# The first product of a fused convolution and feed-forward block: 81 to 80 products a block, with a new order of all queues

## The chip, the core and the metric

The kernel runs on one core of a Trainium2 chip. The core has a matrix engine (TensorE, in the profile PE; its weight loads are PEld), three other compute engines (VectorE DVE, ScalarE ACT, GpSimd POOL) and SyncE (SP), which here issues transfers only. Each engine works through its own queue in order, and the engines wait for one another by semaphores. The metric is the device time of one execution in microseconds (us).

## The reference

`x` has 8 sequences of 4096 tokens with 192 channels. Each channel is convolved along the sequence with 7 taps (a softmax over a row of `weight`, one row for each of 8 groups of 24 channels); then follows a feed-forward block with a SiLU between two matrix products.

```python
def _attn_ref(x, weight):
    ...
    x_unf = x_pad[:, idx, :].reshape(B, S, K, H, group)
    out = np.einsum('hk,bskhg->bshg', w, x_unf)
    return out.reshape(B, S, D).astype(np.float32)

def _moe_ref(x, w_in, w_out):
    h = x @ w_in                          # 32768 x 192 by 192 x 2048
    g = h * (1.0 / (1.0 + np.exp(-h)))
    return (g @ w_out).astype(np.float32) # by 2048 x 192
```

Everything is in 32-bit floats.

## The kernel before

**Blocks.** The 32768 tokens are cut into 32 blocks (`NB`) of 1024 (`TT`), and each block into two halves of 512 (`TB`). The 192 channels are three thirds of 64 (`NK`), and the 2048 hidden features are 16 chunks of 128. Block 0 is computed plainly (`up_plain`, `down_plain`); from block 1 on, both matrix products are computed with fewer multiplications, in the manner of Strassen's scheme: sums of inputs and sums of weights are multiplied, and the results are sums of these products.

**Up products (h).** One product is a matmul with 64 rows (a third of the channels, or a sum of such thirds), 128 columns (a chunk of features, or a sum of chunks) and 512 tokens; it occupies one half of TensorE's rows, the upper or the lower one, and a product in the other half can run beside it. Plainly, a block needs 16 x 3 x 2 = 96 of them. Before, the chunks stand in five groups of three (`GROUPS`), each with 15 products in place of 18, and one chunk stays plain (`plain`, two of its products cut into halves of 256 tokens): 5 x 15 + 6 = 81. `product` adds into one of three banks of a group (`CHAINS`, `CHAIN_BANKS`); `sums_h` makes the outputs out of them: ScalarE copies a bank (`u`), VectorE adds (`X`, `a`, `b`), ScalarE takes the SiLU (`S`).

**Inputs of the up products.** `load` (token `ld`) brings a third of the channels of a block's tokens into `nat` with four transfers of 64 KB; `turn_in` (`i`) transposes it on VectorE into `xt`; `halo_in` (`ha`) fills in the six tokens before each half, with a transfer `xt<-xt` among its steps; `conv` (`v`) computes the taps, the first on ScalarE and six on VectorE, back into `nat`; `spread` (`sp`) copies the result within the chip's SBUF to both halves of the rows (`dup`, eleven transfers a block); `win` (`w`) makes the sums of inputs (six VectorE adds).

**Down products.** `out_slot` (`D`) multiplies with 128 rows and 32 columns, four such tiles side by side, 192 matmuls a block; `sum_g` (`t`) makes its sums of inputs on VectorE (16 a block), `merge` (`z`, `y`, `x`, `M`) its sums of outputs, `turn_out` (`o`) transposes the output on VectorE, `store_out` (`st`) stores it, three transfers of 64 KB each.

**The order.** Nothing is scheduled while the kernel is built: two lists of tokens are written out, `START` for the first blocks and `PLAN` for all others, and every instruction is pinned to its place in its engine's queue (`pin`). `step` reads a token: `P8.3` is product 8 of group 3 of block b; a prefix moves it to another block (`-` one back, `=` two back, `+` one ahead). `ld`, `i`, `ha`, `v`, `sp`, `w` always work for the block after the one named. `PLAN` is gone through 31 times, for b from 3 to 33; what is not there any more is left out. In the old `PLAN`, 48 `D` tokens stand in one stretch, and the products in another. Its input steps stand thus (number of `P` and `L` tokens and of `D` tokens ahead of them): `+ld.1` 0 and 0, `+ld.2` 2 and 13, `+i.2` 19 and 48, `+ld.0` 29 and 48, `+i.1` 48 and 48, `+i.0` 61 and 48.

**Weights.** `combine` makes the sums of weights of a group once, on GpSimd, each operation on 64 rows and 128 columns (19 for a group, 3 more for one of them).

Of the kernel before, what the change touches and what calls it, by code (L numbers as in the profile page):

```python
# [9 lines left out]
F32 = mybir.dt.float32  # L10
# [7 lines left out]
def kernel(  # L18
# [8 lines left out]

# [4 lines left out]
    nc = tc.nc  # L43
# [33 lines left out]

    PLAN = (
        "+ld.1 P5.0 | -P8.3 -S1.4 -a0.2 -S4.3 | -D0.00 -t.01 -S0.2 | -D1.00 -S1.2 =o.2 v.00 "
        "| -D2.01 -t.03 -S5.1 =st.2 | -D2.00 -b5.3 | -D1.20 -sp.0 v.21 -S5.3 | -D4.01 u5.0 "
        "-t.02 -S1.3 | -D5.01 -sp.2 | -D4.00 -t.10 | -D0.20 -t.11 | -D3.01 | -D0.11 -t.12 | "
        "-D1.30 v.22 | -D3.00 +ld.2 -t.13 | -D2.11 -a0.3 | -D5.00 | -D2.10 -t.20 -S0.3 | "
        "-D3.11 v.11 | -D5.10 | -D4.11 -w.0 | -D0.30 v.12 | -D4.10 -t.21 | -D1.11 -t.23 | "
        "-D0.21 | -D0.01 v.23 -w.1 | -D3.10 -t.22 | -D5.21 | -D0.31 | -D5.11 | -D1.10 -t.30 "
        "| -D1.01 -t.31 | -D2.20 | -D2.21 v.13 | -D5.20 | -D4.21 v.01 v.14 | -D4.20 v.24 | "
        "-D1.21 -w.2 | -D3.20 -t.33 | -D2.30 v.02 | -D1.31 -t.32 | -D2.31 -y1.0 | -D5.30 "
        "v.03 | -D0.10 v.25 | -D3.21 -z1.0 v.15 -y0.0 | -D4.31 -y2.0 -w.3 | -D5.31 -M1.0 | "  # L90
        "-D3.30 -x2.1 v.26 -x2.0 | -D4.30 -x2.2 -M2.0 | -D3.31 -w.5 -x0.0 -M3.0 | L.02 | "
        "P2.0 -x2.3 -w.4 | P5.4 | P3.0 u4.0 -M6.0 | L.12 v.16 u5.4 | L.00 | P6.0 -x1.0 -M4.0 "
        "| L.10 u2.0 | P2.4 | L.01 X2.0 | L.11 v.04 u4.4 | P9.0 | P1.0 SL.0 -M5.0 SL.2 | "
        "P6.4 | P13.0 u0.0 X4.0 SL.1 | P5.1 | P3.4 -M7.0 S2.0 +i.2 u2.4 | P0.0 | P7.0 X2.4 | "
        "P11.0 | P12.0 u1.0 a5.0 -o.1 | P9.4 | P1.4 S4.0 b1.0 -st.1 u5.1 | P13.4 | P4.0 X4.4 "
        "u0.4 | P10.0 | P2.1 a1.0 +ld.0 v.05 | P7.4 | P0.4 u4.1 b5.0 | P14.0 | P8.0 u1.4 "
        "v.06 S5.0 | P11.4 | P14.4 a5.4 S3.0 a0.0 S2.4 | P6.1 | P12.4 S3.4 | P4.4 | P3.1 "
        "u2.1 b1.4 S4.4 | P5.2 | P10.4 X2.1 | P1.1 a1.4 u5.2 | P9.1 b5.4 | P2.2 u0.1 | P8.4 "
        "X4.1 | P5.3 u4.2 | P7.1 a0.4 | P0.1 +i.1 u5.3 sp.1 | P12.1 a5.1 | P6.2 u1.1 | P3.2 "
        "-o.0 | P4.1 u2.2 b1.1 | P13.1 | P2.3 a1.1 | P10.1 S2.1 | P1.2 u4.3 X2.2 | P8.1 | "  # L100
        "P11.1 -o.3 u0.2 | P13.2 S1.1 a0.1 | P6.3 S4.1 | P9.2 +i.0 | P0.2 b5.1 u2.3 +ha.0 | "
        "P3.3 S0.0 X4.2 | P1.3 S2.2 | P12.2 u1.2 | P11.2 X2.3 | P7.2 u0.3 b1.2 | P14.1 S4.2 "
        "| P9.3 a5.2 S0.4 | P0.3 -st.0 | P10.2 S1.0 X4.3 | P14.2 u1.3 | P7.3 b5.2 +v.20 "
        "-st.3 | P4.2 S0.1 | P12.3 a5.3 S3.1 | P14.3 +v.10 a1.2 | P13.3 | P4.3 S5.2 b1.3 | "
        "P8.2 S2.3 | P11.3 a1.3 S3.3 | P10.3 S5.4 t.00 S3.2"
    )
    START = (
        "=dp.28 =v.20 =v.10 =dp.44 =v.00 =dp.18 =dp.6 =dp.40 =dp.7 =dp.32 =dp.23 =dp.30 "
        "=dp.13 =dp.2 =dp.20 =dp.24 =dp.15 =dp.35 =dp.14 =dp.33 =dp.11 -ld.1 =dp.37 =dp.36 "
        "=dp.25 -ld.2 =dp.27 =dp.17 -ld.0 =dp.0 =v.11 =dp.34 =v.01 =dp.26 =v.12 =dp.29 =v.21 "  # L110
        "=v.13 =dp.45 =v.22 =dp.21 =v.02 =dp.42 =v.14 =v.03 =dp.39 =v.15 =dp.3 =v.04 =dp.38 "
        "=v.16 =dp.47 =v.23 =sp.1 =v.05 =dp.1 =v.24 =dp.22 -i.1 =dp.12 =v.25 =v.06 =dp.43 "
        "=v.26 =go.2 =sp.0 =dp.19 -i.0 =dp.46 -i.2 =dp.31 -ha.0 =dp.9 =sp.2 =dp.4 =dp.41 "
        "-v.10 -v.00 -v.11 =dp.8 -v.20 -v.01 =dp.5 -v.12 =dp.16 -v.02 =w.0 =dp.10 =w.1 =cp.0 "
        "-L.01 -P5.0 -v.03 =cp.1 -L.02 -P5.4 =w.2 -u5.0 -L.10 =w.3 -u5.4 -P2.0 -P3.0 -v.13 "
        "-P2.4 -u4.0 -v.04 -P6.0 -L.00 -u4.4 -L.12 -u2.0 -L.11 -SL.0 -X2.0 -P6.4 -SL.2 =w.4 "
        "=cp.2 -P9.0 -P1.0 -u2.4 =o.0 -P13.0 -P5.1 -v.14 -u0.0 -X4.0 -P3.4 -P1.4 -S2.0 =w.5 "
        "-SL.1 -P7.0 -P11.0 -u5.1 -X2.4 -u0.4 -P12.0 -P0.0 -a5.0 -v.21 -P13.4 -P0.4 -u1.0 "
        "=o.1 -P4.0 -P9.4 -u1.4 -v.15 -S4.0 -P2.1 -P14.4 -a1.0 -b1.0 -P14.0 -P8.0 -u4.1 -X4.4 "
        "-S3.4 -P6.1 -P10.0 -v.22 -S2.4 -a0.0 -P11.4 -P7.4 -u2.1 -b5.0 -S3.0 -P5.2 -P3.1 "  # L120
        "-S4.4 -a5.4 -P1.1 -P12.4 -u5.2 -X2.1 -P4.4 -u0.1 -P9.1 -b1.4 -P2.2 -a1.4 -P10.4 "
        "-X4.1 -P5.3 -u4.2 -P8.4 =o.2 -P6.2 -b5.4 -P13.1 -u5.3 =st.2 -a0.4 -P0.1 -P7.1 -u2.2 "
        "-v.23 -S2.1 ld.1 -P2.3 -P3.2 -a5.1 -u1.1 -S0.0 -P1.2 -P12.1 -X2.2 -S0.4 -P4.1 -u4.3 "
        "-P13.2 -b1.1 ld.2 -S1.4 -P6.3 -a1.1 -u0.2 -P10.1 -v.24 -P11.1 -u2.3 -P8.1 -b5.1 "
        "-P0.2 -S4.1 -P9.2 -v.05 -S2.2 -a0.1 -P12.2 -P1.3 -u1.2 -X4.2 -S0.1 -P3.3 -P14.1 "
        "-b1.2 -u0.3 -S5.4 -P7.2 -P11.2 -X2.3 -v.16 -P10.2 -P0.3 -S4.2 -a5.2 -sp.1 -P9.3 "
        "-P14.2 -u1.3 -b5.2 -S3.1 -P13.3 -P4.2 -X4.3 -S3.2 -S1.0 i.1 -P14.3 -P12.3 =st.0 "
        "-S1.1 -a1.2 -P11.3 -P7.3 -S5.0 -v.06 -S1.2 -t.00 -D0.00 =st.1 -S3.3 -S2.3 -D1.20 "
        "-b1.3 -S5.1 ld.0 -S4.3 -t.01 -D0.01 -S5.2 -D0.21 -t.02 -D1.11 -sp.0 -a5.3 -D1.10 "
        "-v.25 -t.03 -P8.2 P5.0 +ld.1 -P4.3 -P10.3 -D1.30 -b5.3 -v.26 -D1.00 -a0.2 -sp.2 "  # L130
        "-D4.01 -t.10 -S0.2 -D5.00 -D2.01 i.0 -D4.00 -t.11 -D2.00 i.2 -D5.01 ha.0 -t.13 "
        "-D0.11 -D3.00 -a1.3 +ld.2 -D3.01 -t.12 v.10 -D4.11 -w.0 v.00 +ld.0 -D5.10 v.11 v.20 "
        "-D5.11 -D2.10 u5.0 -t.20 -D0.20 -w.1 -D3.11 -t.21 -D4.10 -w.2 -D2.11 -t.23 -P8.3 "
        "P2.0 -D0.31 -a0.3 -t.22 -D3.10 -S0.3 -S1.3 -D4.21 v.21 -S5.3 u4.0 v.01 -D4.20 -t.30 "
        "-D3.20 -D5.21 -t.31 -D2.20 -D5.20 -D2.21 -D0.10 -t.32 -D2.30 v.02 -D1.01 -t.33 "
        "-D0.30 v.03 -D1.31 v.12 -D2.31 v.04 v.22 -D1.21 v.05 -D3.30 -y1.0 -w.3 -z1.0 -D5.30 "
        "v.13 -D5.31 -D3.31 -x2.0 -M1.0 -x2.1 -D4.31 -x2.2 v.14 -x2.3 -y2.0 -M2.0 -D3.21 "
        "-y0.0 v.06 -D4.30 -x0.0 -w.4 v.23 -x1.0 P3.0 P5.4 -M3.0 L.10 u5.4 -w.5 P6.0 L.02 "
        "-M4.0 L.11 u2.0 L.00 P2.4 X2.0 P1.0 L.01 -M5.0 u4.4 v.15 L.12 u0.0 P6.4 P9.0 SL.2 "
        "SL.0 P0.0 P13.0 X4.0 SL.1 u2.4 -M7.0 P3.4 P5.1 S2.0 +i.0 P7.0 P1.4 u5.1 X2.4 P12.0 "  # L140
        "P11.0 u0.4 a5.0 u1.0 v.24 P9.4 P2.1 S4.0 b1.0 P4.0 P13.4 u4.1 X4.4 P14.0 P10.0 a1.0 "
        "P0.4 P7.4 S3.0 b5.0 v.25 P11.4 P8.0 u1.4 a5.4 S2.4 P6.1 P12.4 a0.0 P14.4 P4.4 u2.1 "
        "b1.4 v.26 P5.3 P3.1 S3.4 a1.4 S4.4 P10.4 P1.1 X2.1 P5.2 P8.4 -M6.0 u0.1 b5.4 P9.1 "
        "P0.1 u5.2 -o.1 u5.3 P13.1 P2.2 X4.1 -st.1 u1.1 +i.2 P12.1 P2.3 u4.2 a0.4 S2.1 P7.1 "
        "P6.2 b1.1 u4.3 P3.2 a5.1 P6.3 u2.2 P10.1 S5.4 X2.2 P4.1 u2.3 S0.4 P9.2 b5.1 P1.2 "
        "S0.0 a1.1 P13.2 P11.1 S1.0 -o.0 u0.2 P8.1 v.16 P1.3 S2.2 S4.1 sp.1 P0.2 P12.2 a0.1 "
        "u0.3 X4.2 S5.0 P3.3 P14.1 u1.2 +i.1 P7.2 P11.2 X2.3 -st.0 b1.2 P9.3 P0.3 S4.2 a5.2 "
        "+ha.0 P10.2 u1.3 X4.3 P4.2 S0.1 P7.3 b5.2 P14.3 S1.1 a1.2 S3.1 P12.3 P14.2 S3.3 a5.3 "
        "P13.3 -o.3 P4.3 S3.2 b1.3 -st.3 +v.10 P8.2 +v.20 a1.3 P10.3 P11.3 S5.2 t.00 S2.3"
    )  # L150
    QUEUE = (0, 4, 1, 2, 3)
    CHAIN_BANKS = ((0, 1, 7, 1, 0), (2, 3, 2, 3, 2), (4, 4, 4, 4, 4))
    PLAIN_BANKS = (7, 4, 3)

# [12 lines left out]
    def bank():  # L167
        return psum.tile([P, TB], F32, tag="ps", name="ps")

# [72 lines left out]
    pool.memset(xts[0][0:R, :, 0:pad], 0.0)  # L242


    WC = 2 * NK * P
    in32 = moe_w_in.bitcast(I32).rearrange("(k r) (a m c) -> r k a m c", r=R, a=2, m=NM)
    out32 = moe_w_out.bitcast(I32).rearrange("(a q e p) d -> a q p e d", a=2, e=2, p=P)
    wr = [const.tile([P, 2, NK, P], F32, name=f"wr{j}") for j in range(NJ)]
    ws = [const.tile([P, 2, NK, P], F32, name=f"ws{j}") for j in range(NJ)]
    wo = [const.tile([P, 2, 2, D], F32, name=f"wo{j}") for j in range(NJ)]  # L250
    wx = [const.tile([P, 3, 2, HD], F32, name=f"wx{j}") for j in range(NJ)]
    raws = {}

    def raw_tile(key):
# [112 lines left out]
    def combine(g, e):  # L367
# [8 lines left out]
        for order in COMBINE[e]:  # L376
            op(*order)
# [733 lines left out]
```

## Time and profile before

| | |
|---|---|
| median of 3 runs | 2348.87 us (2348.78 to 2348.98) |
| the profiled execution: its span | 2347.5 us |
| granted TensorE clock, mean | 1.00 |
| 64-row matmul records of `product`, 64x512 | 4650, mean 593 to 599 ns |
| VectorE add of a bank, 128x512 (`g<-u,ps`) | 465, mean 680 ns |
| ScalarE copy of a bank, 128x512 (`u<-ps`) | 775, mean 586 ns |
| VectorE transposes of the input (L465) | 96, mean 698 ns |

The span and every duration below are those of one execution taken by the hardware profiler. A row of a group reads: line, engine, operation, output and inputs, shape, count, then busy time and mean length of one, then the idle time of the engine right before such instructions and what ended it. Records of an engine overlap a little, since instructions are pipelined; where an engine's next instruction starts before the record of the last one is over, the distance of the starts is what counts. A 32-bit matmul shows as two records.

### The profile page before, as it was taken

The page shows a single profiled execution, that of the slowest core. Times are in us where ns is not written, and L with a number is a line of the kernel's source. Part 1 is how long each engine was busy: PE and PEld are TensorE (multiplying, and loading weights), DVE is VectorE, ACT ScalarE, POOL GpSimd, SP SyncE. Part 2 cuts the span into 40 slices and gives each one's busy share as a digit, 9 for nine tenths or more (in the row PEclk, how much of TensorE's full clock was granted, in tenths as well). Part 3 has the DMA queues.
Part 4 walks back from the last instruction along what each step waited for, and adds up shares of the span by engine and source line. Part 5 has one row for each costly group of instructions (what it writes and reads, how often), then busy time and mean ns, then how long its engine had stood idle before and what let it go on. Part 6 is the DMA issues. An engine that isn't in the chain of part 4 may idle for free.

```text
span 2347.5 us, 43988 instructions
## 1 busy us (share of the span) xinstructions
PE 2340.3 (100%) x17630; PEld 1061.0 (45%) x17630; DVE 2099.6 (89%) x2877; ACT 1187.3 (51%) x2275; POOL 96.8 (4%) x168
## 2 busy tenths in 40 slices
PE   9999999999999999999999999999999999999998
PEld 4344444444444444434444444444444444444445
DVE  8899989899899998998998999989999989899876
ACT  4345644456544466444564445654446644456443
POOL 4920000000000000000000000000000000000000
PEclk9999999999999999999999999999999999999999
DMA  7232212222121221222221222212222212222111
GB/s 158 52 66 48 47 27 47 38 53 53 29 41 36 53 53 31 39 43 46 53 49 31 42 38 53 53 29 42 36 53 53 38 33 45 43 53 44 20 24 25
DMA packets 451245, 106.56 MB, mean 45 GB/s; under 512 B 423584, under 2 KB 428704, under 8 KB 451040
## 3 DMA queue, kind: packets, MB, share of 16 engines
q1 hardware_dynamic: 447392, 101.78, 23.7%
q8 instruction: 138, 2.26, 0.4%
q0 software_dynamic: 448, 1.58, 0.3%
q10 hardware_dynamic: 3200, 0.39, 0.1%
q14 instruction: 67, 0.55, 0.1%
HBM read 31.46 MB, written 25.17 MB: 24 GB/s over the span
## 4 chain that ended last, share of the span: by engine, by line
PE 99%; DVE 0%; ACT 0%; issue 0%; ACTq 0%
PE ps L741 47%; PE ps L625 42%; PE ps L642 5%; PE ps L762 2%; PE ps L571 2%; PE ps L1010 1%; PE ps L423 0%; DVE t L709 0%; ACT g L686 0%; DVE cmb L163 0%; ACT u L163 0%; DVE osb L163 0%; DVE osb L829 0%; DVE g L668 0%; PE ps L449 0%
## 5 line engine op out<-in xcount | busy, mean ns | idle before, releaser
L625 PE MATMUL ps<-win,wr 64*128 64x512 f32 x1550 | 720.3, 597 | 0.0
L741 PE MATMUL ps<-g,wo 128*32 128x512 f32 x2976 | 702.4, 593 | 0.0
L625 PE MATMUL ps<-win,ws 64*128 64x512 f32 x1550 | 631.3, 595 | 0.0
L741 PE MATMUL ps<-t,wo 128*32 128x512 f32 (+2 forms) x4528 | 545.7, 446 | 0.0
L674 ACT COPY u<-ps 128x512 f32<-128x512 f32 x775 | 446.8, 586 | 173.6 <-PE ps L625 161.4
L741 PE MATMUL ps<-t,wx 128*32 128x512 f32 x2976 | 495.5, 592 | 0.1
L625 PE MATMUL ps<-dup,wr 64*128 64x512 f32 x868 | 425.4, 593 | 0.0
L499 DVE SCALAR_TENSOR_TENSOR nat<-xt,taps,nat 128x512 f32<-128x512 f32 x564 | 411.3, 753 | 3.8 <-ACT nat L496 3.6
L686 ACT ACTIVATE g<-g 128x512 f32<-128x512 f32 x465 | 286.1, 633 | 231.5 <-DVE g L668 231.5
L804 ACT COPY yx<-ps 32x512 f32<-32x512 f32 x150 | 86.9, 579 | 574.0 <-PE ps L741 572.3
L709 DVE TENSOR_TENSOR t<-g 128x1024 f32<-128x1024 f32 x248 | 300.6, 1219 | 51.1 <-PE ps L741 43.4
L625 PEld LDWEIGHTS ps<-win,wr 64*128 64x128 f32 x1550 | 275.6, 186 | 150.4 <-issue 67.8
L668 DVE TENSOR_TENSOR g<-u,ps 128x512 f32<-128x512 f32 x465 | 311.2, 680 | 28.8 <-PE ps L625 14.6
L625 PE MATMUL ps<-dup,ws 64*128 64x512 f32 x682 | 324.2, 599 | 0.0
L709 DVE TENSOR_TENSOR t<-g,t 128x1024 f32<-128x1024 f32 x248 | 301.8, 1217 | 12.2 <-PE ps L741 9.4
L741 PEld LDWEIGHTS ps<-t,wo 128*32 128x32 f32 x4528 | 186.7, 110 | 274.1 <-issue 247.6
L625 PEld LDWEIGHTS ps<-win,ws 64*128 64x128 f32 x1550 | 254.7, 186 | 110.5 <-issue 40.8
L686 ACT ACTIVATE g<-ps 128x512 f32<-128x512 f32 x465 | 266.8, 597 | 41.1 <-PE ps L625 38.4
L668 DVE TENSOR_TENSOR ps<-u,ps 128x512 f32<-128x512 f32 x310 | 214.7, 692 | 43.7 <-ACT g L686 19.0
L741 PE MATMUL ps<-g,wx 128*32 128x512 f32 x1488 | 250.5, 592 | 0.0
L741 PEld LDWEIGHTS ps<-g,wo 128*32 128x32 f32 x2976 | 170.2, 110 | 120.9 <-issue 118.9
L741 PEld LDWEIGHTS ps<-t,wx 128*32 128x32 f32 x2976 | 120.5, 110 | 217.5 <-issue 202.3
(90 smaller groups left out, 1764.5 us busy)
## 6 DMA issues: line engine op xcount, KB each, us to landing
dup<-nat SPq DMA_DIRECT2D x345, 128.0 KB, 2.3
nat<-in_x_dram SPq DMA_DIRECT2D x382, 64.0 KB, 2.4
out_dram<-osb SPq DMA_DIRECT2D x376, 64.0 KB, 2.0
raw<-in_moe_w_out_dram SPq DMA_DIRECT2D x8, 384.0 KB, 3.6
raw<-in_moe_w_in_dram SPq DMA_DIRECT2D x12, 192.0 KB, 4.7
ws<-wr POOLq DMA_DIRECT2D x8, 192.0 KB, 5.0
raw<-in_moe_w_in_dram SPq DMA_DIRECT2D x6, 128.0 KB, 3.1
xt<-xt SPq DMA_DIRECT2D x31, 4.5 KB, 1.9
```

The source lines that it names most:

```text
L499: nc.vector.scalar_tensor_tensor(out=dst, in0=src, scalar=tap, in1=dst, op0=ALU.mult, op1=ALU.add)
L571: nc.tensor.matmul(hs[a, n, e], rows(wr[j], e)[:, a, k, :], rows(d, e)[:, n, k, :], start=k == 0, stop=k == NK - 1,)
L625: nc.tensor.matmul(to[:, cols], raw(g, *LEFT[e][r], e), rhs[:, cols], start=first, stop=True, skip_group_check=True,)
L642: nc.tensor.matmul(banks[PLAIN_BANKS[n and 1 + e]][:, cols], rows(wr[j] if own == e else ws[j], e)[:, a, k, :], rows(dups[b], e)[:, SLOT[e ...
L668: pin(nc.vector.tensor_tensor(out_, u, v, op=op))
L674: pin(nc.scalar.copy(us[b, g, o][:, cols], t1[:, cols]))
L686: pin(nc.scalar.activation(h, src, AF.Silu))
L709: pin(nc.vector.tensor_tensor(t[i // 2][:, i % 2, :], u, v, op=ALU.subtract))
L741: nc.tensor.matmul(accs[b][at][SQ * q : SQ * q + SQ, to], lhs[:, e, SQ * k : SQ * k + SQ], rhs[:, e, ts(q, TB // 4) if i == 5 else to], st ...
L762: nc.tensor.matmul(banks[DOWN_BANKS[k]][R * n : R * n + R, :], wo[j][:, a, e, R * k : R * k + R], gs[b, j, a][:, n, e, :], start=j == 0 an ...
L804: pin(nc.scalar.copy(to, acc[3 * (name[0] == "x") + k][n:P, :]))
L1010: nc.tensor.matmul(by_pe[k][n], rows(diag, n)[:, k, i, :], rows(xts[0], n)[:, k, i : i + TB], start=i == 0, stop=i == K - 1,)
```

## The change

The chunks now stand in four groups of four, each with 20 products in place of 24; no chunk is plain: 80 products a block. The sums are a graph over banks: a product adds into one of seven banks of its group (`PRODUCT`: half of the rows, weight, input, bank), and steps named in `MICRO` hand sums on. `c` is a ScalarE copy (with a sign) from a bank into SBUF, into an output `h`, or into another bank, where products go on adding; `a` is a VectorE add or subtraction; `s` is the SiLU on ScalarE. A group has 11 copies, 7 adds and 8 SiLUs. Banks, buffers for copies and the buffers of `t` and `osb` are handed out in order of their first use and given back after a counted number of uses (`at`, `TOUCHES`). One third of the channels is convolved with negated taps from block 1 on (`FLIPS`, `turned`). `combine` makes the sums of two groups at once, 28 operations on 64 rows and 2 x 128 columns. The accumulator of the small down products is cleared by a VectorE memset (`seed`, token `ze`) in place of a matmul's start flag. Both lists are new.

```diff
     PLAN = (
-        "+ld.1 P5.0 | -P8.3 -S1.4 -a0.2 -S4.3 | -D0.00 -t.01 -S0.2 | -D1.00 -S1.2 =o.2 v.00 "
...
+        "ld.2 ld.1 i.1 ld.0 i.2 i.0 i17_f.1 j10.1 k12.3 ha.0 i18_10.1 S16.0 P14.1 h17.3 v.00 P2.3 "
...
+        "k9.3 S14.3 k17.2 P13.3 P15.2 i15_f.3 v.04 k17.3 P12.2 P15.3 P4.3 S20.3 D1.31 D1.01 "
+        "i17_f.2 D1.11 S18.0 S13.3 S18.1 S14.2 j10.2 D1.00 S17.1 i18_10.2 P4.2 S13.2 j10.3 ze.0 "
+        "P14.2 v.20 t.01 P12.3 i18_10.3 P14.3 D2.00 D2.01 t.03 D1.21 S15.1 t.02 D3.00 D3.01 D5.01 "
...
+        "D3.31 D3.30 sp.1 z1.0 x2.1 w.0 x2.3 x2.2 x2.0 y2.0 w.2 w.1 x0.0 w.3 w.4 +P7.0 w.5 +P1.0 "
+        "M1.0 +P7.1 +P1.1 D4.30 +h15.0 M2.0 +k12.0 D4.31 M3.0 +P8.0 +P2.0 +h15.1 +k12.1 +P8.1 "
+        "+h17.0 +P2.1 x1.0 +h17.1 +P18.1 M6.0 +u4.0 +P5.0 +u4.1 M4.0 M5.0 +j4.0 +P17.1 +P5.1 "
+        "+P18.0 +k5.0 +k8.0 +P3.0 +P16.0 +P11.0 +P17.0 +S19.1 +k8.1 +P11.1 +u6.0 +h18.0 +P0.0 "
+        "+u10.0 +P9.0 +P19.0 +j4.1 +P6.0 +P10.0 o.1 +P6.1 +S19.0 +k5.1 +S14.0 +P16.1 +P3.1 +u10.1 "
+        "M7.0 +S20.0 o.2 o.3 +P7.2 +j6.0 +k9.0 +P13.0 +P10.1 st.1 o.0 +i15_f.0 +u6.1 +h18.1 +P4.0 "
+        "+j6.1 +P19.1 +P9.1 +h15.2 +i15_f.1 +k17.0 +P0.1 +P12.0 +j10.0 +P15.0 +S13.0 +k9.1 +P13.1 "
+        "+S14.1 +P7.3 +P4.1 +i17_f.0 +P8.2 +S20.1 +S17.0 +P1.2 +k17.1 +h15.3 +P8.3 +P12.1 +S13.1 "
+        "+u4.2 +P15.1 +k12.2 +P1.3 +i18_10.0 +P14.0 +h17.2 +P5.2 +u4.3 +P17.2 +P2.2 st.3 +P18.2 "
+        "+P5.3 st.0 st.2"
     )
...
+    PRODUCT = {0: (1, 9, 4, 'b1'),
...
+               14: (1, 8, 2, 'b4'),
...
+    MICRO = {'u4': ('c', 'u4', 'b0', None, 1),
...
+             'j6': ('a', 'b0', 'u6', 'b0', 1),
+             'k8': ('c', 'b3', 'b0', None, 1),
...
+             'j10': ('a', 'b4', 'u10', 'b4', 1),
...
+             'S16': ('s', 'h3', 'b4', None, -1),
...
+             'i17_f': ('a', 'h4', 'h4', 'b6', 1),
...
+             'i18_10': ('a', 'h5', 'h5', 'b4', -1),
...
+    FLIPS = (1, 1, -1)
...
+    def at(b, kind, name, g=""):
+        key = (b, name, g)
+        if key not in held_at:
+            held_at[key] = homes[kind].pop(0)
+            touched[key] = 0
+        touched[key] += 1
+        tile_ = held_at[key]
+        if touched[key] == TOUCHES[name]:
+            homes[kind].append(held_at.pop(key))
+        return tile_
...
+    def product(b, r, g):
+        e, w, x_, to = PRODUCT[r]
+        first = r in FRESH and (b, g, to) not in begun
+        begun.add((b, g, to))
+        pin(
+            nc.tensor.matmul(
+                at(b, "bank", to, g),
+                raw(g, w, e),
+                rows(slot_of(b, x_), e),
+                start=first,
+                stop=True,
+                skip_group_check=True,
+            )
+        )
+
+    def micro(b, name, g):
+        kind, to, u, v, sign = MICRO[name]
...
+        seen = {x_: place(x_) for x_ in dict.fromkeys((to, u, v)) if x_}
+        if kind == "c":
+            if sign > 0:
+                pin(nc.scalar.copy(seen[to], seen[u]))
+            else:
+                pin(nc.scalar.activation(seen[to], seen[u], AF.Copy, scale=-1.0))
+        elif kind == "s":
+            pin(nc.scalar.activation(seen[to], seen[u], AF.Silu, scale=float(sign)))
         else:
...
+            op = ALU.add if sign > 0 else ALU.subtract
+            pin(nc.vector.tensor_tensor(seen[to], seen[u], seen[v], op=op))
...
-    for g in (0, 4, 1):
-        for e in range(2):
-            combine(g, e)
+    for e in range(2):
+        combine((0, 1), e)
```

In the new `PLAN` the `D` tokens and the products alternate in six stretches: 26 products, 4 `D`, 4 products, 42 `D`, 4 products, 2 `D`, and 46 products, which run on into the 26 at the head of the next pass. On SyncE's queue the order is `ld.2 ld.1 ld.0 ha.0 sp.0 sp.2 sp.1 st.1 st.3 st.0 st.2`, and on VectorE's the last before the head of the next pass are `o.3 +j6.0 o.0 +i15_f.0 +j6.1 +i15_f.1 +j10.0 +i17_f.0 +i18_10.0`, then `i.1 i.2 i.0 i17_f.1 j10.1 i18_10.1`.

## The prediction

> **What bounds the kernel now.** I read the engines' busy time first, then the chain that ended last, then TensorE's timeline over one block, then SyncE's queue and the groups behind it. The engines:
>
> ```profile
> PE 2340.3 (100%) x17630; PEld 1061.0 (45%) x17630; DVE 2099.6 (89%) x2877; ACT 1187.3 (51%) x2275; POOL 96.8 (4%) x168
> ```
>
> TensorE is never idle, VectorE has 11% to spare, ScalarE half. The chain gives the rhythm of a block of 1024 tokens:
>
> ```profile
> 1191.53 31.00 PE ps L625 x140
> 1222.52 36.22 PE ps L741 x384
> 1263.67 31.00 PE ps L625 x140
> 1294.67 36.22 PE ps L741 x384
> ```
>
> From 1222.52 to 1294.67 is one block, 72.14 us: 36.22 us of down products (L741) and 35.92 us of up products (L625 with L642). The timeline of TensorE gives the price of one product and of a change of kind (start, length):
>
> ```profile
> 1219.36 0.59 PE L625 MATMUL ps<-dup,wr 64*128 64x512 f32 x1
> 1219.79 0.59 PE L625 MATMUL ps<-win,wr 64*128 64x512 f32 x1
> ...
> 1221.93 0.59 PE L625 MATMUL ps<-win,wr 64*128 64x512 f32 x1
> 1222.45 1.07 PE L741 MATMUL ps<-g,wo 128*32 128x512 f32 x8
> ```
>
> A product is two records, 0.43 us from start to start, in one half of the rows; the two halves run side by side. So a pair (one product in each half) takes 0.859 us, a product 0.43. From the last up record to the first down record is 0.52 us where 0.43 would do: a change of tile shape costs 0.09. The 81 products of a block fill 40.5 x 0.859 = 34.79 us; with two changes (0.18) that leaves 0.95 us of small waits in the 35.92.
>
> SyncE issues the transfers one behind the other:
>
> ```profile
> 1270.01 2.12 SPq L181 DMA_DIRECT2D nat<-in_x_dram  x4
> ...
> 1284.76 0.63 SPq L487 DMA_DIRECT2D xt<-xt  x1
> 1285.43 3.31 SPq L838 DMA_DIRECT2D out_dram<-osb  x6
> 1288.79 2.12 SPq L181 DMA_DIRECT2D nat<-in_x_dram  x4
> ```
>
> Ten transfers take from 1285.43 to 1290.91, so 0.548 us each, whatever they wait for. And what waits for the loads, with the rows that the sum below uses:
>
> ```profile
> nat<-in_x_dram SPq DMA_DIRECT2D x382, 64.0 KB, 2.4
> L465 DVE STREAM_TRANSPOSE xt<-nat 128x512 f32<-128x512 f32 x96 | 66.8, 698 | 0.7 <-DMA nat<-in_x_dram 0.7
> L668 DVE TENSOR_TENSOR g<-g,ps 128x512 f32<-128x512 f32 x156 | 105.1, 674 | 4.1 <-PE ps L625 1.0
> ```
>
> A load lands 2.4 us after its issue; in the whole run the transposes of the input waited 0.7 us for it, because `i.0` stands 32 products behind `ld.0` in the old list, and `i.1` and `i.2` further behind theirs.
>
> **The change, part by part.**
>
> *Products.* 80 instead of 81: -0.43 us a block. But the old list keeps all products of a block in one stretch, the new one cuts four out into the down products at two places (`P4.2 P14.2 P12.3 P14.3`, and `+P7.0 +P1.0 +P7.1 +P1.1`). That makes six changes of tile shape in place of two: 4 x 0.09 = +0.36. Together -0.07 a block. If a change cost nothing it would be -0.43, if it cost double, +0.29.
>
> *Small waits.* The scheme hands sums on between banks by ScalarE copies: 44 copies a block for 25, and 28 adds on VectorE for 35. ScalarE gains 19 x 0.586 (the row of `u<-ps`) = 11.1 us, 37 to 48 us of 72; VectorE loses 7 x 0.60 = 4.2 us. Both lie beside TensorE, which is full; uncovered they would cost 11.1 and save 4.2. A ScalarE copy from a bank into a bank has no row; the nearest pair are VectorE's adds, 692 ns into a bank and 680 ns into SBUF, so I take 0.59 (from 0.47, the start-to-start distance of copies, to 0.69). I leave the 0.95 us a block as they are, with 0 and 1.9 as ends. The Trainium skill (ScalarE: Activation LUTs, the tip on ScE to PSUM) says that ScalarE writes PSUM faster than SBUF; it gives no figure, and no row here shows it.
>
> *The head of the list.* The new list ends `... +j6.0 +k9.0 +P13.0 +P10.1 st.1 o.0 ... st.3 +P18.2 +P5.3 st.0 st.2` and begins `ld.2 ld.1 i.1 ld.0 i.2 i.0 i17_f.1 j10.1 k12.3 ha.0 i18_10.1 S16.0 P14.1`. The transposes `i` stand right behind their loads, on VectorE's queue, and behind them three adds that TensorE needs. Let U be the start of the long stretch of products (46 at the end of the list, then 26 at its head).
> - `P6.0` is the 18th product, the ninth pair: it ends at U + 9 x 0.859 + 0.16 (a record outlasts its step by 0.59 - 0.43) = U+7.9. `j6.0` reads its bank (0.60 to the next instruction), then `o.0` transposes the last output (0.70): done at U+9.2.
> - SyncE then has `st.0`, `st.2` (3 + 3 stores) and `ld.2`, `ld.1`, `ld.0` (4 each): 18 transfers. The 18th is issued at 9.2 + 17 x 0.548 = U+18.5 and lands at U+20.9. (`ld.1`, the 14th, lands at U+18.7, so `i.1` and `i.2` are over by U+20.1.)
> - VectorE: `i.0` from U+20.9 (0.62 to the next), `i17_f.1` 0.60, `j10.1` 0.60, `i18_10.1` 0.69: U+23.4, and 0.1 to the matmul: U+23.5. `P14.1` adds into the bank that the last two use.
> - `P14.1` is due behind 46 products, at U + 23 x 0.859 = U+19.76. It is 3.75 us late, and with it the whole queue of TensorE.
>
> Nothing covers this: SyncE's 18 issues take 9.9 us, and between U+14.6 (the add behind `P15.0`, of the 16th pair: 13.9 + 0.69; it is the last ahead of `i.1`) and U+18.7 VectorE has nothing it may run, though work stands behind. What is late next: on ScalarE `v.00` (it waits for the halo transfer of `ha.0`, which SyncE issues behind `i.0`), and behind it copies that TensorE needs; they and VectorE's backlog could add up to 1 us. I take 3.75. Low end: issue at 0.50 (the median of a load's issue alone is 0.487) and landing at the 1.9 minimum: 3.75 - 0.8 - 0.5 = 2.4. High end: 4.75, and 0.6 for slower landings among six stores: 5.35.
>
> The list runs 31 times; in 28 of them a block is left to load. START, which covers the first blocks, puts other work between `ld` and `i`.
>
> *The rest at nothing.* Tap signs by three small GpSimd operations, once. Combining the weights: 28 operations on two chunks at once for a pair in place of 19 to 22 per group; 64x128 took 0.45 us alone and 0.76 in the mean, 128x192 0.59 alone, so about 0.73 to 1.27 for 256 columns: the first pair is done 20 to 36 us after 43.3 (where GpSimd's timeline has the combining begin), ahead of the first product at 102; the second pair by 119 at the latest, its first product comes some 36 products (15 us) after 102. Cover: the plain first block; uncovered 2 us, once. Window sums and spread transfers stay six and eleven a block.
>
> *Sum.* Against the span of 2347.5: 28 x (3.75 - 0.07) + 3 x (-0.07) = +102.8, so 2450.3; the median of the runs lies 1.4 over this profile's span: 2452 us, +4.4%.
>
> **The rivals.**
> 1. *The loads come in time*, because SyncE issues them earlier than I place them or `o.0` is early. For it: the transposes waited 0.7 us in the whole run before. Against it: in the new order 18 issues must pass between `o.0` and the last load's issue. Then 31 x (-0.07) remains, and up to 31 x (-0.95) if the small waits go: 2317 to 2347, 2335 as a middle. It decides where the late time falls from 3.75 to under 0.
> 2. *The clock falls in the wait.* At the end of the run the clock was read so (window, length, busy times, then PEclk):
>
> ```profile
> 2340.00:2341.50 1.50, 1.46 (x25) 0.87 (x16) 0.32 (x2) 1.16 (x5) 0.00 (x0) 1.00 0.95 154
> 2343.00:2344.50 1.50, 0.00 (x0) 0.00 (x0) 0.99 (x3) 0.24 (x1) 0.00 (x0) 1.00 0.66 109
> 2345.00:2345.50 0.50, 0.00 (x0) 0.00 (x0) 0.00 (x0) 0.00 (x0) 0.00 (x0) 0.83 0.79 130
> ```
>
> TensorE stopped at 2341.5 and the granted clock fell at about 2345.2, 3.7 us later. A wait of 3.75 is at that edge. If it falls each time and stays at half for as long again, 1.85 us are lost: 28 x 1.85 = 52 us, 2504. The Trainium skill (TensorE: Matmul & The Clock Gate, Part 1) says the same of an idle window of about 3.4 us, and that the window runs free, so that a wait of 3.75 would hit it only now and then.
> 3. *The hand-overs cost instead.* Loads in time, but each of the 19 more copies a block holds TensorE by 0.10 (records of 0.69 for 0.59 stand in its timeline now): 31 x (1.9 - 0.07) = +57, 2405. Against it: in the old list VectorE's adds, which are longer, stood in the same places.
>
> **How the numbers follow.** Forecast 0.69, first rival 0.14, second 0.12, third 0.05. The time is the forecast's, 2452. Its own ends are 2.4 and 5.35 us a block: 2414 and 2496; the third rival and some falls of the clock widen that to 2400 to 2520, which leaves out the first rival and a tail, under 2 in 10. Within 0.2% (2344.2 to 2353.6, about what a measurement of this kernel can tell from no change) lies a small part of the first rival, 0.02; faster 0.12; slower 0.86.
>
> **What would show it.** In the profile after: TensorE idle some 4 us once a block, some 20 us into the long stretch of products, at 28 places; its weight load there released by VectorE or ScalarE; the input transposes idle before them for some 4 us each block, released by the load of `nat`, against 0.7 us in all now; six stores and twelve loads in one run on SyncE; PEclk 1.00 but for the second rival. The sum is wrong if the idle time stands elsewhere or the transposes find their data.

## The result and the profile after

| | before | after |
|---|---|---|
| median of 4 runs | 2348.93 us (2348.78 to 2349.07) | 2542.36 us (2540.38 to 2546.54) |
| ratio | 1 | 1.0826 (95% interval 1.0810 to 1.0841) |
| span of the profiled execution | 2347.5 us | 2538.7 us |
| granted TensorE clock, mean | 1.00 | 0.98 |
| length of a block in the equal stretch | 72.14 us | 78.02 us (mean of 27) |

The change makes the kernel 8.3% slower. The prediction said slower by 4.4%, 2452 us, in a range up to 2520: sign and place are right, the size isn't. First the engines' busy time and the chain that ended last, by engine, in the page of the kernel after:

```profile
PE 2411.2 (95%) x17382; PEld 1056.1 (42%) x17382; DVE 1984.9 (78%) x2691; ACT 1468.1 (58%) x2833; POOL 100.3 (4%) x129
...
PE 76%; SPq 10%; DVE 8%; DMA 3%; issue 2%; ACT 1%; DVEq 0%; ACTq 0%
```

TensorE is idle for 5% now. The chain, which ran through TensorE alone, passes through SyncE (SPq), VectorE and a transfer in a quarter of the span. One pass of it, in order of time (start, length, what):

```profile
1761.26 8.08 PE ps L642 x36
...
1769.43 0.70 DVE ps L671
1770.13 0.62 DVE t L815
1770.77 0.32 SPq L825
...
1773.31 0.50 SPq L825
1773.85 0.50 SPq L272
...
1779.49 0.31 SPq L272
...
1779.85 2.27 DMA nat<-in_x_dram
...
1782.20 0.71 DVE xt L529
1782.92 0.57 DVE g L671
...
1784.88 13.99 PE ps L642 x51
```

This is the chain that the prediction wrote down, link by link: nine pairs of products up to `P6.0`, the add `j6.0` (L671), the output transpose `o.0` (L815), six stores (L825), twelve loads (L272), a landing, `i.0` (L529), three adds, then TensorE. With U = 1761.19, the start of the stretch, its times stand beside the forecast thus: `o.0` done at U+9.6 (forecast 9.2), last load issued at U+18.6 (18.5), landed at U+20.9 (20.9), TensorE goes on at U+23.7 (23.5). The input transposes waited so in the whole run, against 0.7 us before (the row of their group):

```profile
L529 DVE STREAM_TRANSPOSE xt<-nat 128x512 f32<-128x512 f32 x96 | 64.8, 699 | 160.0 <-DMA nat<-in_x_dram 160.0
```

The last product stretch without a load (from 2461.78) takes 32.26 us, the 27 with one 37.68 in the mean. But 26 products remain at 1784.88, thirteen pairs, and 13 x 0.859 = 11.2 us would do where the chain shows 13.99. The windows over that piece (window, length, busy times of PE, PEld, DVE, ACT and POOL, then the granted clock, the share of the DMA engines and GB/s):

```profile
1786.00:1787.00 1.00, 1.00 (x4) 0.52 (x4) 0.72 (x2) 1.00 (x3) 0.00 (x0) 0.54 0.00 0
...
1789.00:1790.00 1.00, 1.00 (x6) 0.66 (x4) 0.96 (x2) 1.00 (x3) 0.00 (x0) 0.75 0.00 0
1790.00:1791.00 1.00, 1.00 (x7) 0.50 (x5) 0.29 (x1) 0.85 (x3) 0.00 (x0) 1.00 0.00 0
```

When TensorE goes on, its clock falls to half for 3.4 us. The clock did so in 23 of the 27 equal passes, and kept full speed in four. These four let the loss be split: pass by pass, the wait is the distance from the end of the last product's step to the next start, and the rest is what the stretch takes over 32.29 us, its length without a wait. In the four passes at full clock that rest is a backlog: behind the wait the weight loads of the next products are released by ScalarE's copies (L664, L666), the first at U+25.2. ScalarE had itself waited for VectorE's adds (4.04 us in the pass from 668.25).

| per pass, mean of the 27 | us | forecast |
|---|---|---|
| wait of TensorE | 3.75 (3.07 to 5.21) | 3.75 |
| behind it, at full clock (4 passes: 0.70 each) | 0.70 | 0 |
| half clock (23 passes with 1.80 behind the wait in place of 0.70) | 0.94 | 0 |
| the pass without any wait, against 72.14 (from the run with early loads) | 0.48 | -0.07 |
| sum | 5.87 | 3.68 |

Over the 27 passes this is 158.6 us. The other 32.6 lie at the ends: the first of these 27 passes begins 34.5 us later than its counterpart before (355.30 against 320.79), and the end is 1.9 us shorter. The three longest waits in those first 355 us, from TensorE's timeline (in brackets the idle time and what ended it; the clock went to half at each, for 6.8, 6.8 and 10.2 us):

```profile
116.29 2.92 PE L642 MATMUL ps<-dup,w_other 64*128 64x512 f32 x5 [5.76 <-ACT ps L666]
...
162.12 0.65 PE L723 MATMUL ps<-t,wo 128*32 128x128 f32 x8 [6.40 <-DVE ps L691]
...
301.45 1.22 PE L642 MATMUL ps<-dup,w_other 64*128 64x512 f32 x1 [10.56 <-DVE g L671]
```

### The profile page after: what moved, and what is told of

Same layout as the page of the kernel before. It is cut to its first block, busy times and chain, and to the rows that moved or that the text cites. A ratio compares the mean times of both kernels' runs of the same rounds, so it can differ in the third digit from the quotient of the medians.

```text
span 2538.7 us, 43568 instructions
## 1 busy us (share of the span) xinstructions
PE 2411.2 (95%) x17382; PEld 1056.1 (42%) x17382; DVE 1984.9 (78%) x2691; ACT 1468.1 (58%) x2833; POOL 100.3 (4%) x129
## 4 chain that ended last, share of the span: by engine, by line
PE 76%; SPq 10%; DVE 8%; DMA 3%; issue 2%; ACT 1%; DVEq 0%; ACTq 0%
PE ps L723 44%; PE ps L642 32%; SPq L272 6%; SPq L825 3%; DMA nat<-in_x_dram 3%; DVE ps L671 2%; DVE g L671 2%; DVE two L240 1%; DVE nat L563 1%; DVE xt L529 1%; DVE t L815 1%; DVE mh L240 1%; SPq L582 0%; ACT g L668 0%; DMA dup<-nat 0%
## 5 line engine op out<-in xcount | busy, mean ns | idle before, releaser
L642 PE MATMUL ps<-win,w_own 64*128 64x512 f32 x1488 | 687.5, 619 | 0.1
L642 PE MATMUL ps<-dup,w_other 64*128 64x512 f32 x1240 | 527.6, 629 | 113.3 <-DVE g L671 107.5
L723 PE MATMUL ps<-t,wo 128*32 128x128 f32 (+2 forms) x4528 | 519.4, 447 | 6.4 <-DVE ps L691 6.4
L642 PE MATMUL ps<-dup,w_own 64*128 64x512 f32 x1240 | 485.5, 612 | 0.2 <-DVE ps L671 0.2
L642 PE MATMUL ps<-win,w_other 64*128 64x512 f32 x992 | 477.2, 617 | 0.1
L671 DVE TENSOR_TENSOR g<-g,ps 128x512 f32<-128x512 f32 x496 | 331.9, 679 | 122.7 <-PE ps L642 110.7
L563 DVE SCALAR_TENSOR_TENSOR nat<-xt,turned,nat 128x512 f32<-128x512 f32 x558 | 407.3, 751 | 5.2
L671 DVE TENSOR_TENSOR ps<-u,ps 128x512 f32<-128x512 f32 x372 | 254.2, 691 | 134.2 <-PE ps L642 98.8
L642 PEld LDWEIGHTS ps<-win,w_own 64*128 64x128 f32 x1488 | 251.7, 190 | 155.0 <-issue 104.6
L688 DVE TENSOR_TENSOR t<-g 128x1024 f32<-128x1024 f32 x248 | 299.9, 1220 | 11.8 <-PE ps L723 8.0
L642 PEld LDWEIGHTS ps<-dup,w_other 64*128 64x128 f32 x1240 | 214.2, 197 | 222.3 <-DVE g L671 131.9
L688 DVE TENSOR_TENSOR t<-g,t 128x1024 f32<-128x1024 f32 x248 | 301.6, 1217 | 0.5
L664 ACT COPY u<-ps 128x512 f32<-128x512 f32 x372 | 218.9, 593 | 29.7 <-PE ps L642 28.9
```

Source lines behind the costliest of these rows:

```text
L563: nc.vector.scalar_tensor_tensor(out=dst, in0=src, scalar=tap, in1=dst, op0=ALU.mult, op1=ALU.add)
L642: nc.tensor.matmul(at(b, "bank", to, g), raw(g, w, e), rows(slot_of(b, x_), e), start=first, stop=True, skip_group_check=True,)
L664: pin(nc.scalar.copy(seen[to], seen[u]))
L671: pin(nc.vector.tensor_tensor(seen[to], seen[u], seen[v], op=op))
L688: pin(nc.vector.tensor_tensor(t[i // 2][:, i % 2, :], u, v, op=ALU.subtract))
L723: nc.tensor.matmul(acc[SQ * q : SQ * q + SQ, to], lhs[:, e, SQ * k : SQ * k + SQ], rhs[:, e, ts(q, TB // 4) if i == 5 else to], start=firs ...
```

## The experiments

Every ratio is against runs of the kernel before on the same chip, whose medians there were 2349.0 to 2349.2 us.

### What the clock is worth: work in the wait

Zero weights are multiplied into a bank that only TensorE uses at that time, so the sums stay as they are. The first version had eight such matmuls, the second four.

```diff
+    def fill(b):
+        for n in range(8):
+            pin(nc.tensor.matmul(held_at[b, "b0", 3], rows(zeros, 0), rows(slot_of(b, 5), 0),
+                                 start=False, stop=True, skip_group_check=True))
...
         elif name[0] == "P":
+            if token == "P14.1" and 3 <= b <= NB - 2:
+                fill(b)
             product(b, int(name[1:]), *digits)
```

> Eight matmuls with zero weights (0.43 us each, 3.4 us together) are put ahead of P14.1, so that TensorE works through the wait of a pass; nothing else is moved. Theory A (the 2.4 us that a pass loses behind the wait are two things, some 1.0 us of half clock and 1.4 us of backlog on VectorE and ScalarE): the clock stays at 1.00, TensorE still goes on at U+23.7, and 28 x 1.0 = 28 us are saved: 2514 us. Theory B (all 2.4 us are the clock): 28 x 2.4 = 67 us saved, 2475. Theory C (the clock doesn't matter): 2542.

Measured: 2577.3 us, 1.0970 (1.0938 to 1.1002), so slower by 35 us than the changed kernel. The edit was mis-sized: a matmul is two records of 0.43 us, and without a partner in the other half of the rows it takes 0.86. Eight take 6.9 us, 3.1 more than the wait. It shows one thing all the same: TensorE had no wait and no half clock in any equal pass, so the clock falls because of the pause. (The 1.0 and 1.4 of this expectation still counted small waits that the stretch has without a pause too; the table above, and the next expectation, have them taken off.)

> Four zero matmuls ahead of P14.1 in place of eight (3.4 us, since each is two records of 0.43 in one half of the rows: the eight took 6.9). The 27 equal passes of the changed kernel lose 3.75 us waiting, 0.70 in backlog (read where the clock stayed) and 0.94 by the clock in the mean. Theory A (that split): the clock stays at 1.00, the other two remain, 27 x 0.94 = 25 us less: 2517. Theory B (all 1.64 behind the wait is the clock): 44 less, 2498. Theory C (zeros in one half of the rows don't hold the clock): 2542.

Measured: 2520.7 us, 1.0730 (1.0714 to 1.0746): 21.7 us less than the changed kernel, although four matmuls a pass are added and nothing is taken away; A forecast 25. A pass in the chain of waits:

```profile
1748.04 20.42 PE ps L642 x92
1768.46 3.43 PE ps L655 x8
1771.89 12.47 PE ps L642 x52
```

L655 is the filler; 26 products now take 12.47 us where they took 13.99. The clock fell once in the equal passes. More work on the engine that bounds the kernel made it faster; B, which put all 1.64 us on the clock, is out.

### How the clock falls

In the changed kernel the trace's clock record gives the starts of half clock at 1707.58, 1786.08, 1864.59, 1943.10 and 2021.60: 78.51 apart each time, which is 23 x 3.413, although the 27 passes are 76.6 to 79.4 us long. All falls of a run stand on one raster of 3.413 us, and each lasts 3.413 or a multiple (but the last, which the end of the trace cuts off). What decides is how much of a window of this raster TensorE stands idle. With each matmul record counted as busy for its step of 0.43, and from the first product at 100 us on, the clock never fell behind a window with under 0.49 of it idle in any version of this document, it always fell behind one with over 0.60, and in between it went either way. So a pause of 2.39 us could be enough (in the next run), and one of 3.43 could go free (in the changed kernel). The Trainium skill (TensorE: Matmul & The Clock Gate, Part 1) gives a free-running window of 3413 ns, and the trace agrees to the last digit; its idle window that re-throttles is here one in which about half is idle.

### How long the wait is: stores behind the loads

```diff
-        "ld.2 ld.1 i.1 ld.0 i.2 i.0 i17_f.1 ...
+        "ld.2 ld.1 i.1 ld.0 -st.2 i.2 i.0 i17_f.1 ...
...
-        "+P5.3 st.0 st.2"
+        "+P5.3 st.0"
```

> st.2 (three transfers) goes behind ld.0 on SyncE, so 15 transfers in place of 18 stand between o.0 and the last load's landing. Theory A (the chain over SyncE's issues sets the wait, and a shorter wait keeps the clock): TensorE goes on 3 x 0.53 = 1.6 us earlier, at U+22.1, the clock stays 1.00, which gives back 1.0 more: 28 x 2.6 = 73 us, 2469. Theory B (the chain, but the clock falls as before): 28 x 1.6 = 45, 2497. Theory C (something else than SyncE sets the end of the wait): 2542.

Measured: 2474.6 us, 1.0533 (1.0503 to 1.0564); 68 us less, A said 73. The mean wait is 2.03 us, 1.7 shorter for three issues fewer. The clock still fell in five passes, with pauses from 2.39 us on, where A had ruled that out; behind the wait these five passes lost 2.13 us in the mean, the others 0.73. The first pass, which A counted among its 28, gained nothing.

With both stores behind `ld.0` (`-st.0 -st.2` there, and none at the end of the list):

> st.0 and st.2 both go behind ld.0; START and all else as in the changed kernel. Theory A (the chain over o.0 and SyncE): the loads no longer stand behind a transfer that waits for o.0, they are issued from about U+8 on and land by U+17, ahead of U+19.9; no wait, a pass takes 72.6 us as with the loads half a block earlier, and the first pass may gain too: 2380 to 2396. Theory B (the loads come too late all the same, by the landing among stores): a wait of 1 to 2 us stays, 2425 to 2450.

Measured: 2400.9 us, 1.0220 (1.0205 to 1.0235). No pass has a wait, the stretch takes 32.5 us in the mean. B is out; A's estimate is met but for 5 us. The loads no longer stand behind a transfer that waits for `o.0`. The first pass didn't gain: its stores come from START's own list.

### The loads half a block earlier

```diff
-        "D3.31 D3.30 sp.1 z1.0 x2.1 w.0 ...
+        "D3.31 D3.30 sp.1 +ld.2 +ld.1 +ld.0 z1.0 x2.1 w.0 ...
```

> The twelve loads go behind sp.1 on SyncE, some 30 us earlier, from the second pass of PLAN on. Theory A: they land long before the transposes are due, VectorE doesn't wait, a pass takes 72.1 us: 27 x 5.9 = 159 us less, the first pass stays: 2383. Theory B (the hand-overs of the new scheme cost time of their own, which the wait hides now): a pass takes 73 to 75 us even without the wait, 2410 to 2460. Theory C (the loads meet the eleven spread transfers and make them late): a wait of TensorE for win or dup, over 2450.

Measured: 2396.5 us, 1.0201 (1.0171 to 1.0230). A pass of its chain:

```profile
1082.63 32.30 PE ps L642 x144
1114.93 3.57 PE ps L723 x32
1118.50 1.92 PE ps L642 x8
1120.42 31.07 PE ps L723 x336
1151.48 1.92 PE ps L642 x8
1153.40 1.85 PE ps L723 x16
```

The chain is TensorE alone again and nothing in it is wait. The six pieces add up to 72.63 us (72.62 in 24 of the 27 passes), and they show what the scheme itself costs: the down pieces 31.07 + 1.85 + 3.57 = 36.49 for 36.22 before (+0.27), the up pieces 36.14, with 40 x 0.859 = 34.36 in products, so 1.78 of changes and small waits where the old list had 35.92 - 34.79 = 1.13 (+0.65), and one product fewer, -0.43: together +0.49. Theory A is right on the wait; of B's hand-overs 0.5 us a pass is true, far less than its price. C is out.

### START's part

The same edit in START, beside the early loads in PLAN (`ld.*` of the fourth block behind `=st.2` in place of behind `-sp.*`, those of the fifth, `+ld.*`, behind `sp.1`):

> Early loads in PLAN, and in START too: ld.2 ld.1 ld.0 of the fourth block behind =st.2, those of the fifth behind sp.1. Theory A (two of START's three stalls are the same late load: the memset ze.0 behind i.0 on VectorE at 155 us, and the first head of PLAN at 290 us): 7.4 us and 13.1 + 1.4 us go, 2396 - 22 = 2375. Theory B (they are START's taps and copies, not loads): 2396.

Measured: 2378.2 us, 1.0122 (1.0105 to 1.0139). 18 of A's 22 us: the waits at 162 and 301 us are gone, and only the one at 116 is left. START's loads had stood behind spread transfers that wait for VectorE's taps, and the memset `ze.0` (L691) behind `i.0`.

Then also six VectorE taps of the third block (`-v.24 -v.25 -v.03` to `-v.06`) from ahead of the first add to some twenty products later:

> The version with early loads in PLAN and START; and in START six VectorE taps of the third block (v.24 v.25 v.03 to v.06) go from ahead of the first add j4 to some twenty products later. Theory A (VectorE's taps make the first add late, TensorE stands 5.9 us at 110 us): 6 x 0.64 = 3.8 us off that stall and some of the half clock behind it, 2378 - 4 to 6 = 2373. Theory B (ScalarE, busy without a break from 126 to 143 us, sets that stretch): within 2 us of 2378.

Measured: 2375.1 us, 1.0111 (1.0096 to 1.0126). 3.1 us less, between the two theories: the pause of 5.76 us at 116 is gone, one of 2.80 comes at 123, and the stretch of 158 records still takes 43.9 us where 79 products, 39.5 pairs, need 33.9. ScalarE's part in it was not isolated. This is the fastest version of the new scheme in these runs, and it doesn't reach the kernel before.

### Is it enough to move the instructions that wait?

The loads stay late here, and the transposes go further back. First behind `P16.2`, with `ha.0` and `v.00` right behind them:

> The loads stay where they are; i.1, i.2, i.0, ha.0 and v.00 go behind P16.2, fifteen products later. Theory A (the late loads cost only because the transposes stand ahead of i17_f.1, j10.1 and i18_10.1 on VectorE's queue): TensorE no longer waits at U+19.9, a pass takes 72.1 us, 27 x 5.9 = 159 us less and some 13 of the first pass: 2370. Theory B (the late loads hold the block anyhow, because the taps and spread transfers come later now): a new wait in front of the products of the next block, over 2450.

Measured: 2552.9 us, 1.0866 (1.0835 to 1.0898); theory A falls. The chain of one pass:

```profile
1791.47 1.90 DVE xt L529 x3
...
1793.42 1.89 DMA xt<-xt
...
1795.58 0.72 ACT nat L560
...
1796.84 10.09 PE ps L642 x34
```

TensorE now waits 3.2 us at U+24.6: three transposes, the halo transfer, `v.00` on ScalarE, and then a copy that stood behind `v.00`. Then the transposes were spread singly, and `v.00` to `v.03` put behind `P0.2`:

> The loads stay late; i.1 goes behind i15_11.1, i.2 and i.0 behind i15_f.2, and v.00 to v.03 another ten tokens on, behind P0.2, so that ScalarE doesn't meet v.00 before the halo transfer is through. Theory A (only the place of the waiting instructions on their engines' queues costs): no wait of TensorE, a pass takes 72.6 us as with early loads: 2396. Theory B (the late block is short of time anyway): a wait stays, 2430 or more.

Measured: 2578.4 us, 1.0975 (1.0959 to 1.0992); A falls again. The transposes no longer wait (9.3 us in the whole run), but ScalarE (first row) waits for the halo transfer, and VectorE (second row) for ScalarE; each from its engine's timeline:

```profile
1811.87 0.72 ACT L560 ACTIVATE nat<-xt,turned 128x512 f32<-128x512 f32 x1 [1.85 <-DMA xt<-xt]
```

```profile
1812.62 2.33 DVE L563 SCALAR_TENSOR_TENSOR nat<-xt,turned,nat 128x512 f32<-128x512 f32 x3 [2.96 <-ACT nat L560]
```

The adds for TensorE come behind those 2.96 + 2.33 us. At last `v.00` to `v.04` went in among the down products:

> The loads stay late. i.1, i.2, i.0 and ha.0 stand as in the last such version, but v.00 to v.04, which wait for the halo transfer, now come only among the down products (v.00 behind D2.01, the others singly after it). Theory A (in the two versions before, TensorE no longer waited for the transposes but for copies and adds queued behind v.00 on ScalarE, 1.85 us, and behind v.01 to v.03 on VectorE, 2.3 + 3.0 us): no wait is left, a pass takes 72.6 us, and the first pass is better too: 2375 to 2396. Theory B (a block whose loads come this late can't be caught up): 2430 or more.

Measured: 2479.6 us, 1.0554 (1.0536 to 1.0572). With loads as late as in the changed kernel, the long stretch takes 32.25 us, the first pass has lost its 10.56 us wait too, and the clock is full in every equal pass: the wait is a matter of what stands behind the waiting instruction, as A says. But A's time isn't reached, since four more taps among the down products are too much for VectorE there: the stretch of 336 down records takes 33.6 us in place of 31.07, and the island of four products behind it 2.70 in place of 1.92. In the chain between 1750 and 1840 us two kinds of VectorE work, sums `t` (L688) and taps `nat` (L563), hold a third:

```profile
by line: PE ps L642 41.4%; DVE t L688 17.9%; DVE nat L563 16.5%; PE ps L723 9.4%; issue 8.9%; DVE g L671 3.3%; DVE win L593 1.5%; DVE dup L593 1.1%; ACTq L560 0.1%; DVEq L593 0.1%; ACT g L668 0.0%
```

### The same order in the kernel before

In the old PLAN the six issues of two stores and all twelve loads went to the place of `+i.0`, the transposes with them:

```diff
-        ... P9.2 +i.0 | P0.2 b5.1 u2.3 +ha.0 | "
+        ... P9.2 -st.0 -st.3 +ld.2 +ld.1 +i.1 +ld.0 +i.2 +i.0 | P0.2 b5.1 u2.3 +ha.0 | "
```

> The kernel before, unchanged scheme, with the new list's order of SyncE and VectorE put into its PLAN: st.0, st.3 (six transfers), then ld.2 ld.1 i.1 ld.0 i.2 i.0 at the place of i.0. Theory A (the order costs, whatever the scheme): 18 issues x 0.53 = 9.5 us and 2.4 us landing from o.3 on, of which some 4 are covered; VectorE waits about 8 us, TensorE 5 to 7 a pass, and the clock falls: 28 x 6 to 8, 2520 to 2570. Theory B (the 81-product scheme has enough work ahead): below 2400.

Measured: 2659.9 us, 1.1324 (1.1307 to 1.1341), well above A's range; of its waits (engine, line waited for: us in total, times, longest):

```profile
PE ps L625 <- DVE g L668: 228.9, 27, 9.4
...
DVE xt L465 <- DMA nat<-in_x_dram: 215.1, 55, 8.2
```

The old scheme with this order stands still for 8.5 us a pass, and the clock, at 0.95 in the mean, adds to it: 311 us in all. The order costs, not the number of products. (Its stretch of up products takes 47.4 us for 35.9.)

### The islands of four products

With early loads everywhere, the down products that stand around the two islands were moved out, so that a pass has two changes of tile shape:

```diff
-        ... P15.3 P4.3 S20.3 D1.31 D1.01 i17_f.2 D1.11 S18.0 ... P14.3 D2.00 D2.01 ...
+        ... P15.3 P4.3 S20.3 i17_f.2 S18.0 ... P14.3 D1.31 D1.01 D1.11 D1.00 D2.00 D2.01 ...
-        ... w.4 +P7.0 w.5 +P1.0 M1.0 +P7.1 +P1.1 D4.30 +h15.0 M2.0 +k12.0 D4.31 ...
+        ... w.4 D4.30 D4.31 +P7.0 w.5 +P1.0 M1.0 +P7.1 +P1.1 +h15.0 M2.0 +k12.0 ...
```

> The version with early loads in PLAN and START; and the two islands of four products are joined to the long stretch: D1.31 D1.01 D1.11 D1.00 go behind P14.3, D4.30 and D4.31 ahead of +P7.0. Two changes of tile shape a pass in place of six. Theory A (the changes cost 0.12 each and the down products there cover nothing): 31 x 0.47 = 15 us less, 2363. Theory B (the six down products cover the adds and copies between the products around them, 0.6 to 2 us a pass): 2380 to 2425.

Measured: 2547.9 us, 1.0846 (1.0822 to 1.0858). Both theories are out, B by its size. TensorE's timeline, the waits of one pass:

```profile
1007.66 0.69 PE L642 MATMUL ps<-dup,w_other 64*128 64x512 f32 x1 [0.40 <-DVE g L671]
1010.11 1.37 PE L642 MATMUL ps<-dup,w_other 64*128 64x512 f32 x2 [1.32 <-DVE g L671]
1054.04 1.18 PE L642 MATMUL ps<-win,w_own 64*128 64x512 f32 x3 [0.59 <-ACT g L664]
```

A pass takes 78.5 us, 5.9 more than with the islands. Of these, 4.8 us lie among the products, where TensorE pauses for 0.75, 0.56 and 1.48 us and some products beside the pauses run without a partner in the other half of the rows; 1.1 lie among the down products, of which the first run at half clock (their steps are 0.85 us in place of 0.43). The clock falls in each pass, though the longest pause is 1.5 us. The six down products are cover for adds and copies, and 0.47 us of tile changes is a low price for it.

## Why the prediction was wrong, by its own steps

The place and the path of the wait were right. What failed are the sizes of terms beside it: above all the clock, put at nothing in the sum, and START, put at 3.5 us. Each of the two (25 and 31 us) is more than the 22 us by which the time passes the upper end of the range, 2520.

- *The head of the list.* Right, in every link and in its mean: 3.75 us of wait in the mean of 27 passes (the 28th, the first of the list, waited 10.56). It is shown by the loads moved earlier, by one and two stores moved behind, and by the last version with later transposes and taps, in which the loads stay and the wait goes. Two errors cancelled in it: `P14.1` was due at U+20.3, not 19.76 (the stretch has small waits of its own), and the data were there at U+24.1 in the mean, not 23.5, since loads landed later in some passes. That the mean is 3.75 to the digit is luck.
- *What is late next.* "They and VectorE's backlog could add up to 1 us. I take 3.75": taken at nothing, it was 0.70 in the four passes where it can be read alone, in copies of ScalarE that TensorE needs, as named. (`v.00` itself waited for the halo transfer only twice, 7.3 us in all, in START.) This term was mis-sized; the higher value should have been taken, since nothing covers it.
- *The clock.* The step that failed is the reading of the end of the run: TensorE stopped at 2341.5, the clock fell 3.7 us later (the clock record has 2345.33, so 3.9), "a wait of 3.75 is at that edge". One fall shows only when the next boundary of the raster came, not how long a pause may be: counted back from 2345.33, the window from 2341.92 was wholly idle, and of the window before it only 0.46 us, so this fall tests no pause of a length between the two. The second rival got a chance of 0.12; the clock fell in 23 of 27 passes. The price was smaller than rival 2 had it, 1.10 a fall in place of 1.85: with a fall of 3.41 us at half clock 1.71 would be lost, and the backlog of 0.70 then lies partly beside the slow products.
- *Products and small waits.* -0.07 a pass became +0.48: the saved product is there (-0.43), the four changes cost 0.27 among the down products and, by an estimate, 0.2 among the up products in place of 0.36 together, and small waits grew by the other 0.44, a quarter of what rival 3 charged. This size stood in the ends given (0 to 1.9), and costs 15 us over the run. What these small waits are was not isolated. The copy from a bank into a bank, taken at 0.59 without a row, measured 584 ns.
- *START.* "START ... puts other work between `ld` and `i`" was true and not enough. Its three waits and what goes with them cost 34.5 us where the sum had 3.5. Two of them (18 us) are again loads behind transfers that wait, with a memset or adds behind the transposes; they could have been walked as the head was. Some 3 are taps ahead of the first add. The rest, some 13, stays open.
- *At nothing:* ScalarE's extra work (forecast 11.1 us a block; its busy time grew by 280.8 us, some 9 a block) and VectorE's fewer adds lie beside TensorE, as stated: with early loads they can show only in the 0.44.

The miss of 88.4 us (2538.7 against 2450.3) is made up so: 27 x 1.64 = 44 behind the wait (25 of half clock, 19 of backlog), 27 x 0.55 = 15 small waits, 31 START and the first pass, -1.9 the end.

## What to carry to other kernels

A load that comes late costs what stands behind its first reader on that engine's queue; moving the load cost nothing here, where its buffer is free, and moving the reader only helps if everything that hangs on it moves too and the engine has room there. A pause of the matrix engine has a second price in the clock, and it begins well below the length at which one fall was seen: in these runs every pause over 3.43 us was followed by half clock, shorter ones in part, down to 1.5 us where several stood close together. A start-up list is a program of its own, and each of its queues has to be walked as one walks the steady state.

## What had not been expected of the hardware

- The clock falls on a fixed raster of 3.413 us, and windows about half idle are enough (0.49 was the least, and over 0.60 it always fell); in the joined version pauses of at most 1.5 us beside smaller ones brought it down in every pass.
- Matmuls with zero weights in one half of the rows hold the clock: four of them in the pause made the run 21.7 us shorter.
